# Folding the second half of kv into Wo: four PSUM banks in place of three, and another spread of the Wo matmuls of row tiles 0 and 1

## Chip, cores, metric

The kernel runs on one core of a Trainium2 chip. The metric is the device time of one execution in microseconds (us). Every number of a total time below is a median of runs in the fast state, unless it says otherwise. Traces come from one profiled execution each, so positions "in the trace" are those of one execution.

## The reference, cut to what matters

The model is one block with adaptive layer norm: a linear attention part A, then a SwiGLU part B, on 2048 rows of width 1024 with 32 heads of 32.

```python
h = _layernorm(x) * (1 + ca) + sa
x = x + ga * _A_ref(h, A_wqkv, A_wo)      # part A
h = _layernorm(x) * (1 + cb) + sb
x = x + gb * _B_ref(h, B_w_gate, B_w_up, B_w_down)

# inside _A_ref
kv  = einsum('bhsd,bhse->bhde', pk, v)    # 32 x 32 per head
num = einsum('bhqd,bhde->bhqe', pq, kv)
o   = num / den
return o.reshape(B, S, D) @ wo
```

Since `(pq @ kv) @ wo = pq @ (kv @ wo)`, the kernel folds kv into Wo once (`MW = kv @ Wo`, with ga multiplied into Wo earlier) and then multiplies the queries with MW. The change is about how this fold is mixed with the first matmuls of that last product.

## The kernel before, where the change touches it

The program is a list of operations; a helper finds, for each, what it must wait for. For PSUM, the memory that matmuls write to, it goes by whole banks: an operation waits for the last operation on the same bank, if that was one of *another* engine.

```python
for bank in banks:                        # in _Prog.add
    st = self.excl.get(bank)
    if st:
        for e2, d in st.items():
            if e2 != eng:
                deps_add(d)
    self.excl[bank] = {eng: op}
```

The operations of the stage (`PS` has 8 banks of 128 x 512 fp32):

```python
def kvt_mm(half):                         # 32 matmuls of 128x128 into bank 6, then the masked eviction
    for hl in range(4):
        hg = 4 * half + hl
        for dt in range(NDT):
            P.pe("matmul", out=PS[:, 6, hl * 128:(hl + 1) * 128], ...)
    P.dve("tensor_tensor", out=KVT[:, 4 * half:4 * half + 4, :], in0=PS[:, 6, :]..., in1=MASK..., op=ALU.mult)

def m_mm(hg, banks):                      # the fold: two matmuls, each evicted to MW at once
    for nh in range(2):
        i = m_ctr[0]; m_ctr[0] += 1
        bank = banks[i % len(banks)]
        P.pe("matmul", out=PS[:, bank, :], lhsT=KVT[:, hg, :], rhs=WO[:, hg, nh * 512:(nh + 1) * 512], ...)
        dst = MW[:, hg, nh * 512:(nh + 1) * 512]
        if i % 2 == 0:
            P.act("activation", out=dst, in_=PS[:, bank, :], func=ACT.Copy)
        else:
            P.dve("tensor_copy", out=dst, in_=PS[:, bank, :])

WO_BANKS = [2, 3, 1, 0]
def wo_part(st, nh, hgs):                 # row tile st, half nh of the width, head groups hgs
    bank = WO_BANKS[(2 * st + nh) % 4]
    for hg in hgs:
        P.pe("matmul", out=PS[:, bank, :], lhsT=PQT[:, hg, st * 128:(st + 1) * 128],
             rhs=MW[:, hg, nh * 512:(nh + 1) * 512], start=(hg == 0), stop=(hg == NHG - 1))
```

and their order, after the last G group (G is another product of part A; it keeps TensorE busy until then):

```python
wo_part(0, 0, range(4))
wo_part(0, 1, range(4))
kvt_mm(1)
wo_part(1, 0, range(4))
m_mm(4, [4, 5, 7])
wo_part(1, 1, range(2))
m_mm(5, [4, 5, 7])
wo_part(1, 1, range(2, 4))
m_mm(6, [4, 5, 7])
m_mm(7, [4, 5, 7])
...                                       # then the long stream: head groups 4 to 7 of tiles 0, 1; all 8 of tiles 2 to 15
```

The Wo matmuls with head groups 0 to 3 need only the first half of MW, which is ready. So they can stand between the fold matmuls and cover the evictions. For short, I call these matmuls *covers*, and the eight matmuls of `m_mm(4)` to `m_mm(7)` the *fold matmuls*, first to eighth.

## Time and profile before

| | before |
|---|---|
| median time | 831.89 us (3 runs, 831.71 to 832.13) |
| span of the trace | 829.7 us |
| TensorE (PE) busy | 99%, clock 1.0 |
| share of PE in the chain that ended last | 96% |
| stage of the change in the trace | 187.39 to 194.89 us |

These lines are from the page of before: the span, the busy time of PE with its share and number of instructions, and the shares of the chain that ended last.

```profile
span 829.7 us, 9938 instructions
...
PE 819.3 (99%) x4005; PEld 378.6 (46%) x4083; DVE 311.0 (37%) x665; ACT 196.3 (24%) x335; POOL 40.7 (5%) x58
...
PE 96%; DVE 2%; issue 1%; DMA 0%; ACT 0%; POOL 0%; DVEq 0%; ACTq 0%
...
```

TensorE is the limit, and its idle time is in small gaps. So the question for a change of order is which gaps close. The next lines are the timeline of PE in the stage of the change: start, length, engine, operation, output and inputs, number of matmuls merged into the line. `ps<-mw,pqt` are Wo matmuls, `ps<-g,wv` are those of kv, `ps<-wo,kvt` are the fold matmuls, `ps<-h2t,gug` the first gate matmuls of part B.

```profile
...
187.39 1.89 PE L176 MATMUL ps<-mw,pqt 128*128 128x512 bf16 x8
189.12 1.95 PE L176 MATMUL ps<-g,wv 128*128 128x128 bf16 x32
191.12 0.81 PE L176 MATMUL ps<-mw,pqt 128*128 128x512 bf16 x3
191.85 0.61 PE L176 MATMUL ps<-wo,kvt 128*128 128x512 bf16 x2
192.30 0.59 PE L176 MATMUL ps<-mw,pqt 128*128 128x512 bf16 x2
192.73 0.59 PE L176 MATMUL ps<-wo,kvt 128*128 128x512 bf16 x2
193.16 0.59 PE L176 MATMUL ps<-mw,pqt 128*128 128x512 bf16 x2
193.59 0.91 PE L176 MATMUL ps<-wo,kvt 128*128 128x512 bf16 x3
194.66 0.39 PE L176 MATMUL ps<-wo,kvt 128*128 128x512 bf16 x1 [0.16 <-ACT mw L176]
194.89 52.04 PE L176 MATMUL ps<-mw,pqt 128*128 128x512 bf16 x235
246.76 1.89 PE L176 MATMUL ps<-h2t,gug 128*128 128x512 bf16 x8
...
```

Read starts, not lengths: a record of a 128x512 matmul is 0.38 us long, but in a dense stream one starts every 0.216 us (eight from 187.39 to 189.12). The 32 small matmuls take 0.056 us each. The stage has 24 large and 32 small ones, which is 24 x 0.216 + 32 x 0.056 = 6.98 us of work in 7.50 us. (The lines above count 23 large ones: the first of the four after the kv matmuls has no record in this trace. Its slot began at 190.91.) So 0.52 us are lost in this stage, and the wait table of the stretch from 187 to 196 us says to whom (columns: engine, what it was to write, releaser, total us, times, longest). PEld is the loading of a matmul's weights, which carries the matmul's waits:

```profile
...
PEld ps L176 <- ACT mw L176: 1.1, 3, 0.5
...
PEld ps L176 <- DVE kvt L176: 0.4, 1, 0.4
PEld ps L176 <- DVE mw L176: 0.2, 1, 0.2
PE ps L176 <- ACT mw L176: 0.2, 1, 0.2
```

And these lines of the timeline of all engines show the evictions behind it: kv on VectorE (DVE), three lines of copies to MW, and the two weight loads that were held.

```profile
...
191.11 0.69 DVE L176 TENSOR_TENSOR kvt<-ps,mask 128x512 bf16<-128x512 f32 x1 [2.76 <-PE ps L176]
...
192.28 0.60 ACT L176 ACTIVATE mw<-ps 128x512 bf16<-128x512 f32 x1 [6.54 <-PE ps L176]
...
193.36 0.69 DVE L176 CAST mw<-ps 128x512 bf16<-128x512 f32 x1 [0.17 <-PE ps L176]
...
194.01 1.12 ACT L176 ACTIVATE mw<-ps 128x512 bf16<-128x512 f32 x2 [0.27 <-PE ps L176]
194.10 0.10 PEld L176 LDWEIGHTS ps<-wo,kvt 128*128 128x128 bf16 x1 [0.22 <-DVE mw L176]
...
194.66 0.10 PEld L176 LDWEIGHTS ps<-wo,kvt 128*128 128x128 bf16 x1 [0.46 <-ACT mw L176]
...
```

The eviction of kv ends at 191.80, and the first fold matmul goes at 191.85. The seventh is released at 194.10 by the copy on DVE that began at 193.36, the eighth at 194.66 by the copy on ACT that began at 194.01. An eviction begins 0.42 us after its matmul and takes 0.60 (ACT) or 0.69 us (DVE); with 0.05 us to the release, a bank is taken for 1.07 or 1.16 us. That is 5 to 5.4 matmul slots of 0.216 us. With three banks a fold matmul needs the bank of the one three before it, and the last four fold matmuls have no cover among them.

### The profile page before, as it was taken

Reading aid. Unit: us, or ns where it says so; the run is one execution under the profiler, and the core shown is the slowest. Engines: PE = TensorE matmul, PEld = TensorE weight load, DVE = VectorE, ACT = ScalarE, POOL = GpSimd, SP = SyncE. Lnnn points to the kernel's source line nnn. Section 1 sums busy time; section 2 is a strip of 40 time slices with the busy share of each in tenths; the row PEclk is TensorE's granted clock in tenths of the full one; section 3 lists DMA queues with packets and bytes.
Section 4 is the critical chain, followed back from the end, with each engine's and each line's share of the span. In section 5 each row is a group of like instructions: output and inputs, shape, how many; then the busy total and the mean of one; then the engine's idle time right before and its main releaser. Section 6 shows DMA issues by size and latency. Waiting matters only on the chain.

```text
span 829.7 us, 9938 instructions
## 1 busy us (share of the span) xinstructions
PE 819.3 (99%) x4005; PEld 378.6 (46%) x4083; DVE 311.0 (37%) x665; ACT 196.3 (24%) x335; POOL 40.7 (5%) x58
## 2 busy tenths in 40 slices
PE   8999999999999999999999999999999999999998
PEld 4544444454444444444444444444444444444444
DVE  5797986756955521121221112122111111111111
ACT  3757641323232111111111101111110111111011
POOL 1010000000130000030000003000000300000000
DMA  9969656928297995700455571045557004553000
GB/s 321 289 151 231 148 156 172 202 102 304 56 248 233 283 264 153 197 25 13 123 152 152 152 188 34 13 125 152 156 150 192 26 16 125 152 154 88 0 26 26
DMA packets 199247, 119.29 MB, mean 144 GB/s; under 512 B 57881, under 2 KB 182945, under 8 KB 199201
## 3 DMA queue, kind: packets, MB, share of 16 engines
q1 hardware_dynamic: 199184, 118.65, 52.7%
q8 instruction: 32, 0.52, 0.3%
q14 instruction: 15, 0.11, 0.0%
q10 hardware_dynamic: 16, 0.00, 0.0%
HBM read 100.67 MB, written 4.33 MB: 127 GB/s over the span
## 4 chain that ended last, share of the span: by engine, by line
PE 96%; DVE 2%; issue 1%; DMA 0%; ACT 0%; POOL 0%; DVEq 0%; ACTq 0%
PE ps L176 96%; DVE acc L176 1%; DVE stats L176 0%; DMA xres<-in_A_x_dram 0%; DVE pkt L176 0%; DVE e L176 0%; DVE xres L176 0%; DVE pqt L176 0%; POOL rstd L176 0%; DVE mv L176 0%; ACT mw L176 0%; ACT e L176 0%; DVE ve L176 0%; DVE ut L176 0%; DVE ht L176 0%
## 5 line engine op out<-in xcount | busy, mean ns | idle before, releaser
L176 PE MATMUL ps<-h2t,guu 128*128 128x512 bf16 x879 | 210.3, 379 | 0.9
L176 PE MATMUL ps<-h2t,gug 128*128 128x512 bf16 x878 | 209.9, 379 | 0.9
L176 DVE TENSOR_TENSOR at<-sg,ps 128x512 bf16<-128x512 bf16 x112 | 77.0, 687 | 284.8 <-PE ps L176 274.9
L176 ACT ACTIVATE sg<-ps 128x512 bf16<-128x512 f32 x112 | 66.9, 597 | 309.7 <-PE ps L176 298.3
L176 PEld LDWEIGHTS ps<-h2t,guu 128*128 128x128 bf16 x896 | 87.7, 98 | 105.7
L176 PEld LDWEIGHTS ps<-h2t,gug 128*128 128x128 bf16 x896 | 87.6, 98 | 105.5
L176 PE MATMUL ps<-wd_a,at 128*128 128x512 bf16 (+2 forms) x518 | 113.0, 372 | 0.5
L176 PE MATMUL ps<-ht,wqk 128*128 128x512 bf16 x499 | 110.5, 379 | 1.0 <-DVE ht L176 0.3
L176 PE MATMUL ps<-wd_b,at 128*128 128x512 bf16 (+2 forms) x388 | 85.3, 372 | 0.4
L176 PEld LDWEIGHTS ps<-wd_a,at 128*128 128x128 bf16 x528 | 51.0, 98 | 59.8
L176 DVE TENSOR_TENSOR ut<-att,gb_b 128x512 bf16<-128x512 bf16 (+1 forms) x32 | 14.1, 440 | 167.0 <-ACT att L176 167.0
L176 PEld LDWEIGHTS ps<-ht,wqk 128*128 128x128 bf16 x512 | 49.4, 98 | 58.6 <-issue 0.2
L176 ACT ACTIVATE att<-ps 128x512 bf16<-128x512 f32 (+1 forms) x32 | 17.4, 591 | 182.1 <-PE ps L176 182.1
L176 PEld LDWEIGHTS ps<-wd_b,at 128*128 128x128 bf16 x396 | 38.3, 98 | 44.7
L176 PE MATMUL ps<-pk,xres 128*128 128x512 bf16 x250 | 56.0, 379 | 0.4 <-issue 0.2
L176 PE MATMUL ps<-mw,pqt 128*128 128x512 bf16 x250 | 55.7, 379 | 0.3
L176 POOL TENSOR_SCALAR h2t<-h2t,modcol 128x512 bf16<-128x512 bf16 x32 | 26.4, 843 | 383.2 <-DMA h2t<-xn 383.2
L176 ACT ACTIVATE e<-ps 128x512 bf16<-128x512 f32 x56 | 33.2, 604 | 31.7 <-PE ps L176 20.7
L176 PEld LDWEIGHTS ps<-mw,pqt 128*128 128x128 bf16 x256 | 24.9, 98 | 29.9 <-DVE xres L176 0.4
L176 PEld LDWEIGHTS ps<-pk,xres 128*128 128x128 bf16 x256 | 24.8, 98 | 30.1 <-DVE g L176 0.4
L176 ACT ACTIVATE junk<-xres 128x1024 bf16<-128x1024 bf16 x24 | 25.4, 1058 | 35.5 <-DVE xres L176 35.2
L176 DVE SCALAR_TENSOR_TENSOR xres<-ps,xres 128x512 bf16<-128x512 f32 x32 | 21.5, 688 | 12.2 <-PE ps L176 12.0
(102 smaller groups left out, 339.4 us busy)
## 6 DMA issues: line engine op xcount, KB each, us to landing
gug<-in_B_w_gate_dram SPq DMA_DIRECT2D x56, 512.0 KB, 4.0
guu<-in_B_w_up_dram SPq DMA_DIRECT2D x56, 512.0 KB, 5.3
xres<-in_A_x_dram SPq DMA_DIRECT2D x20, 256.0 KB, 7.8
rb<-recip_den SPq DMA_DIRECT2D x8, 512.0 KB, 11.5
stgx<-in_w_mod_dram SPq DMA_DIRECT2D x2, 2048.0 KB, 8.0
wd_a<-in_B_w_down_dram SPq DMA_DIRECT2D x4, 1024.0 KB, 7.9
out_dram<-xres SPq DMA_DIRECT2D x31, 128.0 KB, 1.7
xres<-in_A_x_dram SPq DMA_DIRECT2D x3, 1024.0 KB, 14.1
```

Source lines behind the costliest of these rows:

```text
L176: return getattr(e, method)(**kw)
```

## The change

Its intent is to remove these waits: bank 6, which is idle once kv is evicted, joins the rotation, and the sixteen covers are dealt out differently. Five, not four, stand between kv and the first fold matmul, and one stands between the sixth and the seventh. No instruction is added or removed.

```diff
         wo_part(0, 0, range(4))
-        wo_part(0, 1, range(4))
+        wo_part(0, 1, range(2))
         kvt_mm(1)
-        wo_part(1, 0, range(4))
-        m_mm(4, [4, 5, 7])
-        wo_part(1, 1, range(2))
-        m_mm(5, [4, 5, 7])
-        wo_part(1, 1, range(2, 4))
-        m_mm(6, [4, 5, 7])
-        m_mm(7, [4, 5, 7])
+        wo_part(0, 1, range(2, 4))
+        wo_part(1, 0, range(3))
+        m_mm(4, [4, 5, 7, 6])
+        wo_part(1, 0, (3,))
+        wo_part(1, 1, (0,))
+        m_mm(5, [4, 5, 7, 6])
+        wo_part(1, 1, range(1, 3))
+        m_mm(6, [4, 5, 7, 6])
+        wo_part(1, 1, (3,))
+        m_mm(7, [4, 5, 7, 6])
```

## The prediction

> **What bounds the kernel now.** TensorE: the page gives PE 99% busy at full clock, and the chain that ended last is 96% PE. The change touches one short stage, from the end of the G groups (187.39 us) to the long stream of Wo matmuls (194.89 us), of a span of 829.7 us.
>
> **The loss in it, from the timeline.** Eight 128x512 matmuls run from 187.39 to 189.12, a slot of 0.216 us each; 32 small kv matmuls take 0.056 us each. The stage's 24 large and 32 small ones need 24 x 0.216 + 32 x 0.056 = 6.98 us. It lasts 7.50 us. The loss, 0.52 us, sits here:
> - 0.1 us before the first Wo-fold matmul (191.85), which waits for the masked eviction of kv on VectorE (from 191.11, 0.69 us). Four Wo matmuls (0.86 us) don't quite cover it.
> - 0.1 us before the seventh fold matmul (194.10, released by a VectorE copy) and 0.32 us before the eighth (194.66, released by a ScalarE copy). With three banks, a fold matmul needs the bank of three before; the last four go back to back, but an eviction starts 0.43 us after its matmul and takes 0.60 us (ScalarE) or 0.69 us (VectorE), so a bank is held for about 1.1 us.
>
> The wait table agrees: weight loads waited for ScalarE mw three times, VectorE mw once, VectorE kvt once.
>
> **What the change does.** It adds and removes no instruction. Bank 6, idle once kv is evicted, joins the rotation, so a fold matmul needs the bank of four before. Five Wo matmuls (1.08 us), not four, cover the kv eviction, and the covers between the four fold pairs become 2, 2, 1 in place of 2, 2, 0. The Trainium skill ("Perfetto Trace Analysis", Optimizing Tensor Performance) says that matmul groups should rotate through different PSUM banks so that evictions overlap the next matmuls; the waits above agree.
>
> Replaying the new order with these durations: fold pairs start at 191.55, 192.41, 193.28 and 193.92; kv is ready 0.14 us early; every bank is free at least 0.3 us early; evictions of one engine start no closer than their own length, so no queue grows. The long stream begins at about 194.35 in place of 194.89. One new edge: its fourth matmul reads the half of mw whose ScalarE copy ends at about 195.0, just when it is due; up to 0.1 us may be lost. The first residual add also comes nearer to the landing of its x tile (issued from 186.5, 9.3 us to landing), but the four-bank ring gives it about 2 us.
>
> **On the critical path:** all of it. PE is the chain before and after, and later waits are short and not for DMA. The gain should reach the end: 0.52 less 0 to 0.1, about 0.45 us.
>
> **Predicted time: 831.4 us**, 831.05 to 831.8 eight times in ten; the runs of before spread over 0.4 us by themselves. Faster by over 2%: 0.2%; within 2%: 99.6%; slower by over 2%: 0.2%.
>
> **What would show it.** In the stage's wait table, waits of PE and weight loads for mw sum to 0.1 us at most, and none is for kvt; the last fold matmul starts at about 194.1, not 194.66; the long stream and the first gate matmuls (246.76 before) start about 0.5 us earlier after the G groups. Evictions keep 0.60 and 0.69 us.
>
> **What would make it wrong.** The stream's fourth matmul waiting longer; the x tile landing late enough to hold PE's bank ring; a later wait (VectorE residual adds around 229 us, one stall of under 0.1 us now) growing; or runs differing by more than the gain.

## The result, and the profile after

The changed kernel took 831.38 us (median of 6 runs, 831.12 to 831.85), the kernel before in the same rounds 831.80 us (6 runs, 831.57 to 832.81). The ratio of the two is 0.9994, with a 95% interval of 0.9981 to 1.0006. A ratio is the mean time of one kernel's fast runs over that of the other's of the same rounds, so it is not quite the ratio of the medians. The interval holds 1: by total times alone, the gain is not shown. The traces have to show it.

The same three lines of the page of after:

```profile
span 829.4 us, 10016 instructions
...
PE 824.2 (99%) x4083; PEld 379.2 (46%) x4083; DVE 310.3 (37%) x665; ACT 196.3 (24%) x335; POOL 40.7 (5%) x58
...
PE 96%; DMA 2%; DVE 1%; SPq 0%; ACT 0%; issue 0%; POOL 0%; ACTq 0%
...
```

A trap is here: PE busy has risen by 4.9 us while the kernel got no longer. The trace of before has 4005 matmul records and this one 4083, which is the number of weight loads in both. So 78 records were missing before, and busy sums of PE can't be compared between these two traces. (It is the trace and not the kernel: the second trace of before, below, has 4083 records and 824.3 us, the second of after 4005 and 818.9 us.) Starts can. The 2% of DMA in the chain of after is mostly the z row's round trip through DRAM, which landed late in this trace; it lies ahead of the stage. The timeline of PE in the stage after:

```profile
...
187.62 1.46 PE L176 MATMUL ps<-mw,pqt 128*128 128x512 bf16 x6
188.91 1.95 PE L176 MATMUL ps<-g,wv 128*128 128x128 bf16 x32
190.70 1.24 PE L176 MATMUL ps<-mw,pqt 128*128 128x512 bf16 x5
191.78 0.59 PE L176 MATMUL ps<-wo,kvt 128*128 128x512 bf16 x2
192.21 0.59 PE L176 MATMUL ps<-mw,pqt 128*128 128x512 bf16 x2
192.64 0.59 PE L176 MATMUL ps<-wo,kvt 128*128 128x512 bf16 x2
193.07 0.59 PE L176 MATMUL ps<-mw,pqt 128*128 128x512 bf16 x2
193.51 0.59 PE L176 MATMUL ps<-wo,kvt 128*128 128x512 bf16 x2
193.94 0.38 PE L176 MATMUL ps<-mw,pqt 128*128 128x512 bf16 x1
194.15 0.59 PE L176 MATMUL ps<-wo,kvt 128*128 128x512 bf16 x2
194.59 52.04 PE L176 MATMUL ps<-mw,pqt 128*128 128x512 bf16 x240
246.47 1.89 PE L176 MATMUL ps<-h2t,gug 128*128 128x512 bf16 x8
...
```

To compare two traces, take lengths of stretches that hold the same work. All runs below are read by the *stretch* from the first Wo matmul after the G groups to the first gate matmul. It holds the whole stage and the long stream, and the work in it is the same.

| stretch (us) | before | after |
|---|---|---|
| start of the trace to first Wo matmul | 187.39 | 187.62 |
| first Wo matmul to long stream (the stage) | 7.50 | 6.97 |
| long stream to first gate matmul | 51.87 | 51.88 |
| the two together (*the stretch*) | 59.37 | 58.85 |
| first gate matmul to the end of the span | 582.99 | 582.97 |

The stage is 0.53 us shorter and at its sum of matmul slots, 6.98 us. Nothing after it gives any of it back. The spans differ only by 0.3 us, since in this one trace the part ahead of the stage, which the change does not touch, was 0.23 us longer.

What is left of waits in the stage, in the wait table of after:

```profile
...
DVE xres L176 <- DMA xres<-in_A_x_dram: 0.6, 1, 0.6
PEld ps L176 <- ACT mw L176: 0.3, 1, 0.3
PEld ps L176 <- DVE kvt L176: 0.2, 1, 0.2
```

Two weight loads still count as waiting, and VectorE now waits for an x tile. None of these costs PE time. The lines for the longest of them, in order ACT copy, Wo matmuls, weight load:

```profile
...
194.57 0.60 ACT L176 ACTIVATE mw<-ps 128x512 bf16<-128x512 f32 x1
...
194.80 0.81 PE L176 MATMUL ps<-mw,pqt 128*128 128x512 bf16 x3
195.22 0.11 PEld L176 LDWEIGHTS ps<-mw,pqt 128*128 128x128 bf16 x2 [0.32 <-ACT mw L176]
```

The fourth matmul of the long stream is the third of the merged line: 194.80 + 2 x 0.216 = 195.23. Its weight load was held to 195.22 by the copy (0.32 us since the load before), and the matmul still went in its slot. The time that PEld stood idle is not the time that PE lost. The Trainium skill ("TensorE: Matmul & The Clock Gate", Architectural detail) says that a matmul can begin before its weight load completes; the trace agrees, with a load of 0.10 us recorded from 195.22 and a matmul started at 195.23.

### The profile page after: what moved, and what is told of

The parts are those of the page before. It is cut to its first block, busy times and chain, and to the rows that moved or that the text cites. A ratio compares the mean times of both kernels' runs of the same rounds, so it can differ in the third digit from the quotient of the medians.

```text
span 829.4 us, 10016 instructions
## 1 busy us (share of the span) xinstructions
PE 824.2 (99%) x4083; PEld 379.2 (46%) x4083; DVE 310.3 (37%) x665; ACT 196.3 (24%) x335; POOL 40.7 (5%) x58
## 4 chain that ended last, share of the span: by engine, by line
PE 96%; DMA 2%; DVE 1%; SPq 0%; ACT 0%; issue 0%; POOL 0%; ACTq 0%
PE ps L176 96%; DMA z_row<-zr 1%; DMA zb<-z_row 0%; DVE stats L176 0%; DMA xres<-in_A_x_dram 0%; DVE mhl L176 0%; SPq L176 0%; DVE xres L176 0%; DVE pqt L176 0%; POOL rstd L176 0%; DVE g L176 0%; DVE mv L176 0%; ACT gtmp L176 0%; ACT e L176 0%; DVE ve L176 0%
```

## The experiments

The theory: two kinds of PE wait were in this stage, 0.42 us for banks and 0.10 us for kv; the order of instructions sets both, and all that is saved reaches the end. The rivals: the fourth bank is the whole gain; the order is the whole gain; or the difference is scatter, or is absorbed by later slack. All kernels gave correct results. The clock was 1.0 in all traces but one, and that is said.

### The changed kernel and the kernel before again

> The changed kernel, unaltered, on another occasion. The measure for all runs is the stretch from the first Wo matmul after the G groups to the first gate matmul (before: 187.39 to 246.76, 59.37 us; after: 187.62 to 246.47, 58.85 us). My theory (the gain is the removal of two kinds of PE wait in this stage, set by the order of instructions): the stretch is 58.85 us again, within 0.03, while the start of the stage may shift by some tenths, as it did between the first two traces (187.39 and 187.62). Total about 0.4 us below the kernel before of the same rounds, 0.2 to 0.7. Rival (the difference is run-to-run scatter): the stretch itself varies by several tenths, and the totals of the same rounds do not differ.

> The kernel before, unaltered, for a second trace of it. Theory: stretch 59.37 us again within 0.03, with the waits of 0.1, 0.1 and 0.32 us in the same places, while the start of the stage moves by some tenths. Rival (scatter): the stretch moves by a tenth or more.

Measured: the stretch of after was 58.84 us (first trace 58.85), that of before 59.37 us (first trace 59.37). In the second trace of before, the fold matmuls stood at the same places to 0.01 us. The stage began at 188.32 and at 187.79 us, so its start moved by up to 0.7 us between traces of the same kernel, while the stretch moved by 0.01. In all twelve traces of this document the part behind the stretch lasted 582.97 to 582.99 us, while the first G matmul, well ahead of the stage, came anywhere from 126.46 to 127.88 us: most of the scatter of the spans lies there. Totals: after 831.47 us (5 runs, 831.06 to 831.87), before 831.82 us (9 runs), ratio 0.9994, interval 0.9981 to 1.0006, as in the first rounds. The second trace of before was of a single run (831.88 us). The rival "scatter" falls for the stretch, and it explains the totals: the runs of after lie 0.7 to 0.8 us apart in each set of rounds, those of before 0.95 to 1.25 us.

### Half of the change: the banks alone

```diff
 # kernel before, its order kept, all four calls
-        m_mm(4, [4, 5, 7])
+        m_mm(4, [4, 5, 7, 6])
```

> Order of before, but bank 6 joins the rotation (four banks). My theory, replayed with the traced durations: the bank waits before the seventh and eighth fold matmul (0.1 and 0.32 us) go; the 0.1 us before the first fold matmul (kv eviction) stays; and since the four last fold matmuls now go back to back, the fourth matmul of the long stream waits about 0.1 us for the ScalarE copy. Stretch 59.04 us (58.97 to 59.12), 0.33 below before. Rival 'the bank is the whole gain': 58.85. Rival 'the order is the whole gain': 59.37. Total 0.3 us below before, about the size of the scatter.

Measured: stretch 58.99 us, from 187.92 to 246.91. The last four fold matmuls in one line, then the first gate matmuls:

```profile
...
194.12 1.03 PE L176 MATMUL ps<-wo,kvt 128*128 128x512 bf16 x4
...
246.91 1.89 PE L176 MATMUL ps<-h2t,gug 128*128 128x512 bf16 x8
```

The first fold matmul stood where it had stood before (4.46 us after the first Wo matmul), the seventh and eighth followed with no gap, and the fourth of the long stream was 0.05 us late. So the banks alone bring 0.38 us. Total 831.61 us against 831.82 us (ratio 0.9996, interval 0.9983 to 1.0010), not resolved.

### Half of the change: the order alone

```diff
 # kernel after, its order kept, all four calls
-        m_mm(4, [4, 5, 7, 6])
+        m_mm(4, [4, 5, 7])
```

> Order of after, but three banks 4, 5, 7. My theory: no wait for kv, no wait before the seventh fold matmul, but the eighth still waits for its bank, 0.2 us. Stretch 59.08 us (59.0 to 59.15), 0.29 below before. So each half alone brings over half of the gain, and the halves overlap. Rival 'the bank is the whole gain': 59.37. Rival 'the order is the whole gain': 58.85. Total 0.3 us below before.

Measured: stretch 59.06 us. The last pair of fold matmuls takes 0.81 us, where it takes 0.59 in after:

```profile
...
193.94 0.81 PE L176 MATMUL ps<-wo,kvt 128*128 128x512 bf16 x2
...
```

The first seven fold matmuls stood where they stand in after, and the eighth was 0.21 us late. So the order alone brings 0.31 us. Total 831.28 us against 831.82 us (ratio 0.9993, interval 0.9981 to 1.0006). By the median it even looks faster than the whole change, which the stretches rule out: another sign that totals can't order these kernels.

Both rivals that give one half the whole gain fall. The halves overlap: 0.38 + 0.31 is more than 0.52, because the one cover ahead of the last pair and the fourth bank each remove part of the same wait.

### The kv wait brought back alone

```diff
 # kernel after
-        wo_part(0, 1, range(2))
+        wo_part(0, 1, range(3))
         kvt_mm(1)
-        wo_part(0, 1, range(2, 4))
+        wo_part(0, 1, (3,))
```

> The kernel after, but one Wo matmul moved back ahead of the kv matmuls, so that four rather than five cover the eviction of kv; banks and the other covers as after. Theory: this brings back just the kv wait, 0.07 to 0.1 us, and no bank wait. Stretch 58.93 us (58.90 to 58.97) against 58.85. Rival (the kv wait of before had another cause, such as weights that load late): 58.85.

Measured: stretch 58.94 us (one look, single run of 831.07 us). The loss of 0.09 us is all ahead of the first fold matmul; the other seven keep their distances from it to 0.01 us. So the kv wait is one of cover alone, and five matmuls are what its eviction needs.

### The bank wait made larger: one bank

```diff
 # kernel before, its order kept, all four calls
-        m_mm(4, [4, 5, 7])
+        m_mm(4, [4])
```

> Order of before, all eight fold matmuls in bank 4 alone, so each waits for the eviction of the one before: the suspected wait made large. My theory: a bank is held 0.42 us to the start of the eviction, then 0.60 (ScalarE) or 0.69 (VectorE), then 0.05 us to the release, 1.07 or 1.16 us in all, so the first fold matmul to the eighth take 7.8 us in place of 2.8. Stretch about 64.3 us (64.0 to 64.6), and the total 5.0 us above before (4.5 to 5.3), since nothing later hides it. Rival (later slack absorbs losses in this stage, so that the stage's gain does not reach the total): stretch and total rise by clearly less than the stage does, or by different amounts.

Measured: total 839.67 us (4 runs, 838.43 to 840.46) against 831.82 us, ratio 1.0091 (1.0077 to 1.0105). The stretch was 66.82 us, 7.45 longer than before. It is a miss: I had expected 5.0. The timeline of PE shows what was missing from the sum:

```profile
...
196.72 0.39 PE L176 MATMUL ps<-wo,kvt 128*128 128x512 bf16 x1 [0.35 <-DVE mw L176]
197.80 0.61 PE L176 MATMUL ps<-wo,kvt 128*128 128x512 bf16 x1 [0.69 <-ACT mw L176]
199.19 0.61 PE L176 MATMUL ps<-wo,kvt 128*128 128x512 bf16 x1 [0.79 <-DVE mw L176]
200.49 0.61 PE L176 MATMUL ps<-wo,kvt 128*128 128x512 bf16 x1 [0.69 <-ACT mw L176]
...
```

A matmul record is 0.39 us long up to 196.72 and 0.61 us from 197.80 on. The table by stretches shows the cause (busy time and number of instructions of each engine, granted clock of TensorE, DMA share, GB/s):

```profile
...
192.20:197.20 5.00, 2.82 (x10) 0.71 (x9) 1.38 (x2) 1.25 (x3) 0.00 (x0) 1.00 1.05 390
197.20:200.90 3.70, 1.62 (x4) 0.35 (x5) 0.69 (x1) 1.14 (x2) 0.00 (x0) 0.57 1.05 387
200.90:203.00 2.10, 2.10 (x6) 0.75 (x5) 0.77 (x2) 0.00 (x0) 0.00 (x0) 0.50 1.05 386
203.00:205.00 2.00, 2.00 (x7) 0.80 (x6) 1.07 (x3) 0.00 (x0) 0.00 (x0) 0.62 0.66 242
...
```

The granted clock fell to half from about 197.7 us to about 204.5 us. (Its mean from 203 to 205 us is 0.62: 0.5 up to about 204.5 and 1.0 after.) All four runs of this kernel show it: their mean clocks are 0.994 to 0.998, those of every other run here 1.000. The long stream took 53.68 us in place of 51.87, so 1.8 us of the surplus are its first matmuls at half clock; the rest, 0.6 us, lies at the last three fold matmuls (from the first fold matmul to the long stream 8.68 us, where the run with filled gaps, below, takes 8.07). The Trainium skill ("TensorE: Matmul & The Clock Gate", Part 1) tells of this gate: half rate after an idle window, full rate after some 3.4 to 4 us of sustained work. The trace agrees on the two rates and on the return (dense work from 200.49, full clock again near 204.5). As to what sets it off, the page's table of why it matters warns of idle gaps of over about 3 us, and no gap between PE records here was longer than 0.8 us. But Part 1 also tells of a kernel that cycled through PSUM banks, in which short idling between groups of matmuls made the clock swing, and that is what is seen here: TensorE was busy for only 2.82 of 5.00 us by its records, and for 1.9 us by its nine slots. The clock record of the trace also shows a step. The half clock lasted 6.83 us, from 197.70 to 204.53, after 191.15 us and before 634.88 us of full clock: 2, 56 and 186 times 3.413 us. In the step of 3.41 us before the fall five matmuls started (1.1 us of slots). That the load within such a step decides is inferred from this, and no run tests it alone.

### A smaller dose: two banks

```diff
 # kernel before, its order kept, all four calls
-        m_mm(4, [4, 5, 7])
+        m_mm(4, [4, 5])
```

> Order of before, two banks 4 and 5 for the eight fold matmuls: a smaller dose than one bank, in which the waits are spread over gaps of 0.1 to 0.5 us and TensorE stays over 80% busy. In the run with one bank the granted clock fell to half and added 2.5 us to the 5.0 us of waits. Theory: the held time of a bank (1.07 or 1.16 us) sets the waits, and the clock falls only where TensorE idles for most of several microseconds. Then here the clock stays at 1.00, the fold matmuls lose 1.40 us in place of 0.49, the stretch is 60.27 us (60.1 to 60.45), and the total 0.9 us above before (0.6 to 1.2). Rival (any added gap also costs clock): the stretch is over 61 us, with matmul slots of 0.43 us.

Measured: stretch 60.31 us, clock 1.000, total 832.66 us (5 runs, 832.60 to 832.93) against 831.82 us; ratio 1.0009 (0.9997 to 1.0022), which holds 1. Medians differ by 0.84 us where the stretch differs by 0.94. The hold time of a bank gives the waits, and gaps alone do not cost clock at this density: its sparsest step of 3.41 us had nine matmul starts (1.9 us of slots).

### One bank, with the gaps filled

```diff
 # kernel of the run with one bank, in m_mm, after the fold matmul
+                for _ in range(0 if hg < 4 or i == 15 else 3 if nh == 0 or hg >= 6 else 2):
+                    P.pe("matmul", out=PS[:, 6, :], lhsT=PQT[:, 0, 0:128], rhs=PQT[:, 0, 0:512], start=True, stop=True)
```

> The run with one bank, plus 19 matmuls whose results nobody reads, two or three after each fold matmul but the last, written to the idle bank 6: they fit in the gaps in which TensorE waited for bank 4, so the waits for the bank stay as they were. Theory (of the 7.45 us that one bank cost, 4.9 us are bank waits and 2.5 us are the granted clock, which fell to half because TensorE idled most of the time): the clock stays at 1.00, the long stream takes 51.87 us again, the stretch is 64.3 us (64.15 to 64.5) in place of 66.82, and the total 4.95 us above before (4.6 to 5.3): more work, yet 2.5 us faster than one bank alone. Rival (the slow matmuls came from something else in that stage, such as the bank itself or the loads running at the same time): the stretch stays near 66.8 us or grows.

Measured: stretch 64.41 us, long stream 51.87 us, clock 1.000, total 836.92 us (5 runs, 836.58 to 837.43) against 831.85 us, ratio 1.0061 (1.0047 to 1.0075). The last matmuls of its stage, fold matmuls with fillers (`ps<-pqt`) between:

```profile
...
198.00 0.39 PE L176 MATMUL ps<-wo,kvt 128*128 128x512 bf16 x1
198.22 0.81 PE L176 MATMUL ps<-pqt 128*128 128x512 bf16 x3
199.17 0.39 PE L176 MATMUL ps<-wo,kvt 128*128 128x512 bf16 x1
...
200.25 0.39 PE L176 MATMUL ps<-wo,kvt 128*128 128x512 bf16 x1
```

The fold matmuls are 1.08 and 1.17 us apart, which is the hold time of a bank. With 19 matmuls more, the kernel is 2.75 us faster by the median than with one bank and no filler (in other rounds, with before at 831.85 and 831.82 us), and the stretch 2.41 us shorter. The rival, that the bank or the loads slowed the matmuls, falls. This run also answers whether a loss in this stage reaches the end: the stretch grew by 5.04 us over before, and the median total by 5.07 us. Nothing later absorbs it.

### The new wait for the x tile taken away

```diff
 # kernel after
-        P.dma("stgx2", STGX[1][:], wmv[:, :, 5120:6144])
         for st in range(4):
             P.dma("xr%d" % st, XRES[:, st, :], xv[:, st, :])
+        P.dma("stgx2", STGX[1][:], wmv[:, :, 5120:6144])
```

> The kernel after, but the first four x tiles are queued ahead of the 2 MB load of w_mod. In the trace after, the first residual add waited 0.6 us for its x tile, a wait that before did not have. Theory: that wait is off the critical path, since PE needs the bank again only about 2 us later. So the wait for DMA goes, and the stretch stays 58.85 us within 0.03. Rival (the tile's landing holds PE back): the stretch gets shorter by 0.05 us or more.

Measured: VectorE no longer waited for a DMA there (before the first residual add it was idle for 0.25 us, released by PE), and the stretch was 58.84 us. So the wait was off the critical path. The run's total was 832.25 us, a single run whose stage began at 188.70 us, the latest start of all traces. It shows the scatter ahead of the stage and nothing of the edit.

### A version meant to beat both

Two more PE waits stood in the traces: up to 0.25 us when the z row's round trip through DRAM lands late (it varies from run to run), and 0.08 us near 229 us, where VectorE is behind because of a reduction of 2.28 us.

```diff
 # kernel after; z_row() is defined further up
+        add(s3, 14, lambda: z_row())
         add(s3, 14, macc_split)
 ...
-            if g == 0:
-                z_row()
 ...
-            if st == 8:
+            if st == 9:
                 mod_red()
                 mod_fin_col(3, False)
 ...
-            if st == 8:
+            if st == 9:
                 th2_mod()
```

> A version meant to beat both: the kernel after, with two more waits of PE aimed at. The z row's round trip through DRAM is started one projection group earlier (before: its landing lets PE pass the sixth G group with 0 to 0.25 us lost from run to run), and the reduction for the second modulation moves one row tile later in the Wo stream (VectorE is behind there, and PE loses 0.08 us near 229 us). Theory: from the first G matmul to the first Wo matmul 60.75 us or less in place of 60.83 to 61.08, no wait of PE for g; stretch 58.77 us in place of 58.85, unless VectorE falls behind at the new place. Total 0.1 to 0.2 us below the kernel after, not resolved by these rounds; 0.5 to 0.7 below before.

Measured: stretch 58.77 us, and no PE wait for g or for the residual adds was left in the wait table. From the first G matmul to the first Wo matmul it took 60.71 us. Of the difference to 60.83, about 0.11 us is only that the two z matmuls moved ahead of the mark, so the undisturbed case (60.83, in eight of the twelve traces) has gained nothing; the edit removes just the late landings (60.94 in the first trace of before, 61.08 in that of after). Total 831.07 us (5 runs, 830.97 to 831.29) against 831.82 us for before, ratio 0.9991 (0.9977 to 1.0005). It has the lowest median of the kernels run with rounds, but after did not run in the same rounds (831.38 and 831.47 us in others), and the interval holds 1. By the stretch it beats both; by total times this stays open.

## Why the prediction was right

- **The time.** Predicted 831.4 us, measured 831.38 us. It was right on the stage, and lucky on the last digit: runs of this kernel lie 0.7 us apart.
- **The size of the loss.** Predicted 0.52 us from the sum of matmul slots; the stretch of two traces of each kernel shortened by 0.52 to 0.53 us.
- **The places.** Relative to the first Wo matmul, the replay put the four fold pairs at 4.16, 5.02, 5.89 and 6.53 us; the trace has them at 4.16, 5.02, 5.89 and 6.53 us. kv was ready 0.13 us early (predicted 0.14). No queue of evictions grew.
- **The two halves.** The bank alone 0.38 us and the order alone 0.31 us, where the same replay gave 0.33 and 0.29.
- **The new edge.** "Up to 0.1 us may be lost" at the fourth matmul of the long stream: its weight load was held to the moment it was due, and nothing was lost. So the gain was 0.52 us and not 0.45. In the run with the banks alone, where the load comes later, 0.05 us was lost there.
- **The x tile.** VectorE did wait 0.64 us for it, as the prediction feared, and the four banks that the Wo matmuls rotate through absorbed it; with the tile loaded first the stretch did not change.
- **All of it on the critical path.** Shown with a larger dose: 5.04 us in the stretch, 5.07 us in the total. For the 0.52 us itself, the traces show that nothing behind the stretch gives it back; totals show a difference of the right sign and size (medians 0.42 and 0.35 us, in two sets of rounds) without resolving it.
- **Where it failed in part.** The check I named was wrong: "waits of PE and weight loads for mw sum to 0.1 us at most, and none is for kvt". The wait table after has 0.3 us for mw and 0.2 us for kvt. They are idle time of the weight loader, which is idle for 0.12 us between two loads of any dense stream (a load of 0.10 in a slot of 0.216), and a load may be held without the matmul losing its slot. The starts of matmuls are the check.

The advice to rotate groups through PSUM banks (the Trainium skill, "Perfetto Trace Analysis", Optimizing Tensor Performance) holds here, with 0.38 us for the fourth bank. But the number of banks is only half of it: an order with one more cover and three banks had 0.31 us.

## What to carry to other kernels

Count what a bank is held for, in matmul slots (here 1.07 to 1.16 us, 5 to 5.4 slots): a matmul waits when fewer slots than that lie between it and the last use of its bank, and another bank or other matmuls put between them are two ways to the same end. Judge a change of tenths of a microsecond by the length of a stretch with fixed work in the traces (it repeated to 0.01 us), not by total times (here up to 1.35 us apart within one set of rounds), and read matmul starts rather than busy sums or idle weight loads. Where gaps make TensorE sparse for several microseconds, the clock can add to what the gaps cost: with one bank the gaps cost 5.0 us and the clock 2.4 us more.

## What the Trainium skill lacked or had wrong

- "TensorE: Matmul & The Clock Gate" (the table of why it matters) warns of idle gaps of over about 3 us. Part 1 tells as well that short idling between matmul groups can make the clock swing, but gives no measure of how sparse is too sparse. Here the granted clock fell to 0.50 with no gap between PE records of over 0.8 us, after about 5.5 us in which nine matmuls ran (nine slots of 0.216 are 1.9 us), five of them in the last 3.41 us. Nineteen filler matmuls in the same gaps kept it at 1.00 and shortened the stretch by 2.41 us. With two banks, some 1.4 us lost in 8.4, and nine matmuls in the sparsest 3.41 us, it stayed at 1.00.
- "Perfetto Trace Analysis" (Optimizing Tensor Performance; Matmul Optimizations) says to rotate through banks and to use all eight, but not how to tell how many suffice. Here a bank is held 0.42 us to the start of the eviction, 0.60 (ScalarE) or 0.69 us (VectorE) for it, and 0.05 us to the release; against the changed kernel, the order of before was longer by 5.56 us with one bank (gaps filled), 1.46 with two, 0.52 with three and 0.14 with four, about 0.09 of each for kv.
- "Perfetto Trace Analysis" (Identifying the Most-Contended Engine) says that matmul busy time is a bad measure; the section does not say that records can be missing. Two traces of the same kernel (before) had 4005 and 4083 matmul records and busy sums of 819.3 and 824.3 us, against 4083 weight loads in both.
- No page that I read tells that idle time of the weight loader is not lost matmul time: a load with 0.32 us of idle time before it, where 0.12 us is usual in a dense stream, cost its matmul nothing.
